# One small job moved from VectorE to ScalarE, the last copies out of PSUM divided between the two, and one last store on GpSimd's queue

## The chip, the cores and the metric

The kernel runs on one core of one Trainium2 chip. The metric is the device time of one execution in microseconds; the time before is the median of three runs, 212.61 us (212.39 to 212.65). Engines are named as in the profile: PE is TensorE, DVE is VectorE, ACT is ScalarE, POOL is GpSimd, SP is SyncE. Each engine works through its own instructions in the order in which the kernel writes them, and waits where an operand isn't ready. A transfer is issued from the queue of SP, ACT or POOL. PSUM is the memory that PE writes its sums to; here it is used as four buffers of two banks each, two with the tag A and two with the tag B.

## The reference

Two independent layers on 2048 positions and 576 channels, their results side by side in the output.

```
# A: 32 heads of 18, each position attends to itself and 7 earlier ones, 2 apart
qkv = x @ wqkv
logits = einsum(q, k[pos - 2*w]) / sqrt(18)      # w = 0..7, masked where pos - 2*w < 0
a = (softmax(logits) weighted sum of v[pos - 2*w]) @ wo

# B: a short shift convolution, a long convolution by FFT, a gate
kv = (sum over t < 4 of k[pos - t] * shift_k[:, t]) * v
y  = irfft(rfft(kv, 4096) * rfft(ssm_k, 4096))[:2048] + kv * ssm_D
b = q * y
out = concat(a, b)
```

## The kernel before

**Layer B.** The 2048 positions are four blocks of 512, and so is the filter ssm_k. For a block i of kv and a block m of the filter the kernel makes a spectrum each (x_spectrum, L776 and L778; filter_spectrum, L627 and L695), as three rows of numbers: two parts and their sum. The output block j is the sum over i of the products of block i with filter block j - i. The products are one DVE multiplication each (L1099). They are summed on PE with identity matrices (sum_of, L1126); the two sums of a block and a third of the channels are copied from PSUM to SBUF by ACT (L1139), and brought back to positions by PE (inverse, L1158 or, for the last third of the last block, last, L1177 and L1185). gate_last multiplies the last block by q on DVE (L1167), in a lower and an upper half of its buffer, and store_b writes each half out as soon as it is made: L1080 the one, L1083 the other in two transfers. The very last of all these sums, for j = 3, t = 2, r = 1, is copied by DVE (L1137) and not by ACT.

**The filter.** Before its spectrum is made each filter block m is folded (fold_filter): two PE groups (L673) into two buffers, two ACT copies of 128x576 (L676) back over the block, and then three accumulating DMAs from POOL's queue (L678, L680, L681). The last of them adds one row of 1x576, the block's row 0 times -0.707, to row 0 of another tile. That signed row is made by negate (L657), for blocks 3 and 2 in the fourth step of the taps' loop, for blocks 1 and 0 between two steps of the attention's logits. Blocks are loaded by transposing DMAs on SP's queue (L227), blocks 3, 2, 1, 0 in this order. L676 overwrites row 0 of blocks 3 and 2, from which their signed rows are made.

**Layer A.** The projections (project, L378, L382, L389, L395; the tail of 64 channels is ct = 4) are copied out of PSUM by ACT (L414). Logits are DVE products (L832) that PE sums (L847); the weighted sum of v is DVE (L956) and PE (L973); the output projection is L1029.

**The order of the work** is written out. PE work that nothing waits for yet stands in a list of units; until() takes as many of them as a table says (PLACES) each time that the kernel waits for a DVE result, need() takes units until a named kind is done. A planner keeps three clocks, D for DVE, P for PE and A for ACT; dve() and pe() advance them. They decide when a gate is due (due) and whether an inverse in the list is ready, and nothing else. The kernel's tile framework adds the waits; it doesn't change the order.

The fourth step of the taps' loop does, in this order: the taps of block 3 on DVE, negate(3, 2), until(), which takes four units, the folds of kv (mirror, L606 on PE into both B buffers and two L609 on ACT), and fold 3, for which need() first takes the units ahead of it.

The store of the last block, by queue: L1080 is issued from SP; of the two L1083 one is issued from ACT and one from SP.

Of the kernel before, what the change touches and what calls it, by code (L numbers as in the profile page):

```python
# [11 lines left out]
ACT = mybir.ActivationFunctionType  # L12
ALU = mybir.AluOpType
# [40 lines left out]
def view(t, offset, dims):  # L54

    return bass.AP(tensor=t.tensor, offset=t.offset + offset, ap=[list(t.ap[0])] + [list(d) for d in dims])
# [3 lines left out]
def kernel(  # L60
# [13 lines left out]
    nc = tc.nc  # L74
    Bsz, S, D = A_x.shape
# [4 lines left out]
    outf = out.flatten_outer_dims()  # L80
# [17 lines left out]
    NBL, BL = 4, 512  # L98
# [20 lines left out]
    def bank2(name, tag):  # L119
        return pp.tile([128, 2, 512], FP32, name=name, tag=tag)  # L120
# [65 lines left out]
    def k_at(m, part):  # L186
        return 3 * HB * (3 - m) + HB * part

    def kTok(m):
        return view(Ks, k_at(m, 2), [[D, 4], [1, D]])  # L190
# [133 lines left out]
    clk = {"D": 0.0, "P": 0.0, "A": 0.0}  # L324
    psum = {"A": deque([0.0, 0.0]), "B": deque([0.0, 0.0])}

    def dve(n, fn, ready=0.0, ns=0.53):

        fn()
        clk["D"] = max(clk["D"], ready) + n * ns / 1000 + 0.125  # L330
        return clk["D"]

    def pe(us, tag, evac, ready=0.0, first=True, last=True):

        clk["P"] = max(clk["P"], ready, psum[tag].popleft() if first else 0.0) + us
        clk["A"] = max(clk["A"], clk["P"] + 0.1) + evac
        if last:
            psum[tag].append(clk["A"])
        return clk["A"]
# [231 lines left out]
    def taps(i):  # L571
        kj, vt = kjs[i], vts[i]
        kv = kv_of(i)
        pair = [view(tB, 4 * D * n, [[D, 4], [1, D]]) for n in range(2)]

        def mult(to, row, n):
            dve(2304 * n, lambda: nc.vector.tensor_tensor(  # L577
                to, view(kj, row * D, [[D, n], [D, 4], [1, D]]), view(skb, row * D, [[D, n], [0, 4], [1, D]]), ALU.mult))

        def add(o):  # L580
            dve(2304, lambda: nc.vector.tensor_tensor(kv, kv if o else pair[0], o or pair[1], ALU.add))

        both = view(tB, 0, [[4 * D, 2], [D, 4], [1, D]])
        if i == 0:
            mult(view(kv, 0, [[4 * D, 1], [D, 4], [1, D]]), 3, 1)
            mult(view(tB, 0, [[4 * D, 1], [D, 4], [1, D]]), 2, 1)
            add(pair[0])
            mult(both, 0, 2)
            add(pair[0])
            add(pair[1])  # L590
        else:
            mult(both, 0, 2)
            add(None)
            mult(both, 2, 2)
            add(pair[0])
            add(pair[1])
        return dve(2304, lambda: nc.vector.tensor_tensor(kv, kv, vt[:], ALU.mult))
# [34 lines left out]
    def row(m, c):  # L632
        return kTok(m)[0:1, c, :]
# [10 lines left out]
    ROOT = 1.4140625  # L644

    def minus_of(m):
        return (view(Ks, k_at(1, 0) + D * (1 + m), [[1, D]]) if m else view(xw, 11 * HB + 2 * D, [[1, D]]))[0:1]

    def spare(m):
        return view(Ks, k_at(1, 0) + D * m, [[1, D]])[0:1]  # L650
# [3 lines left out]
    def negate(*ms):  # L654
        for m in ms:
            signed.add(m)
            dve(288, lambda: nc.vector.tensor_scalar(minus_of(m), spare(m) if m < 2 else row(m, 0), -0.5 * ROOT, None,  # L657
                                                     ALU.mult))

    def fold_filter(m):  # L660
        kt, swapped = kTok(m), m < 2
# [60 lines left out]
    for i in range(NBL):  # L722
        r = taps(i)
        if i == 3:
            negate(3, 2)
# [27 lines left out]
        for n, u in enumerate(mirrors):  # L753
            n = AT[n] if n < 2 else AT[i]
# [153 lines left out]
    logits_run[0] = True  # L908
    sa = softmax(0, view(av, 2048, [[1, 1024]]), view(av, 3072, [[1, 512]]))
    order = [la] * 3 + [partial(negate, 1, 0)] + [la] * 7 + [lb, sa, lb, lb, lb, sa, lb, sa]  # L910
    for n, step in enumerate(order):
        for at in REGROUP:
# [153 lines left out]
    def Y(j, r):  # L1066
        return view(*((av, Y0 + (j % 2) * 8 * D + r * 4 * D) if j else ((av, 0), (xw, 8 * HB))[r]), [[D, 4], [1, D]])
# [4 lines left out]
    def upper(t, j, a, width, c0, n):  # L1072

        return bass.AP(tensor=t.tensor, offset=t.offset + (BL * j + 320 - 64 * a) * width + c0,
                       ap=[[width, 64], [(64, 192)[a] * width, 2], [1, n]])

    def store_b(j, c0, n, src, h):
        other = nc.scalar if j == NBL - 1 else nc.sync
        if h == 0:
            nc.sync.dma_start(outf[BL * j:BL * j + 256, D + c0:D + c0 + n].rearrange("(c p) d -> p c d", c=2), src[:, 0:2])  # L1080
            return
        for a, eng in enumerate((other, nc.sync)):
            eng.dma_start(upper(outf, j, a, 2 * D, D + c0, n), src[64 * a:64 * a + 64, 2:4])  # L1083
# [22 lines left out]
    def sums(j, t, group):  # L1106

        until()
        for i, pr, ready in group:
            out = sum_of(j, t, i, pr, ready)  # L1110
        return out

    def sum_of(j, t, i, pr, ready):

        m = j - i
        for r in range(2):
            sign = ((1, 1), (-1, 1), (-1, -1), (1, -1))[m][r]
            terms = ((2, ident if sign > 0 else identn), (1 - r ^ (m & 1), identn2 if sign > 0 else ident2))
            if i == 0:
                acc[r] = bank2("ps_z", "B")  # L1120
                clk["P"] = max(clk["P"], psum["B"][r])
            for n, (part, w) in enumerate(terms):
                for s in range(2):
                    for h in range(2):
                        o = 64 * ((h + s) % 2)
                        nc.tensor.matmul(view(acc[r], 512 * h, [[192, 2], [96, 2], [1, 96]])[o:o + 64], w[64 * h:64 * h + 64, 64 * h:64 * h + 64],  # L1126
                                         pr[64 * h:64 * h + 64, part, :].rearrange(
                                             "p (a g e) -> p g a e", a=2, g=4)[:, 2 * s:2 * s + 2],
                                         start=(i == 0 and n == 0), stop=(i == j and n == 1),
                                         tile_position=(64 * h, o))  # L1130
            clk["P"] = max(clk["P"], ready) + 0.34
        if i == j:
            for r in range(2):
                y, z = (Y(j, r)[:, :, TH * t:TH * t + TH].rearrange("p (a b) d -> p a b d", a=2),
                        view(acc[r], 0, [[512, 2], [TH, 2], [1, TH]]))
                if (j, t, r) == (NBL - 1, 2, 1):
                    nc.vector.tensor_copy(y, z)  # L1137
                else:
                    nc.scalar.activation(y, z, ACT.Copy)  # L1139
                out = pe(0.0, "B", 0.85)  # L1140
            return out
# [4 lines left out]
    def inverse(j, c0, n, ready):  # L1146
# [17 lines left out]
        def gate_last(lo, hi):  # L1164
            qB = qBs[j][:, :, c0:c0 + n]
            for s, src in enumerate((lo, hi)):
                dve(2 * n, lambda: nc.vector.tensor_tensor(qB[:, 2 * s:2 * s + 2], src, qB[:, 2 * s:2 * s + 2], ALU.mult),  # L1167
                    clk["P"])
                store_b(j, c0, n, qB, s)
# [23 lines left out]
        def back():  # L1193
            ps = bank2("ps_back", "A")
            for src, w in ((A, flip2), (y, flipn)):
                for c in range(2):
                    for h in range(2):
                        o = h ^ (1 - c)
                        nc.tensor.matmul(ps[64 * o:64 * o + 64, 1 - c, 0:n], quarter(w, h, 1),
                                         src[64 * h:64 * h + 64, c], start=(src is A), stop=(src is y),  # L1200
                                         tile_position=(64 * h, 64 * o))
            r = pe(0.0009 * n, "A", ev, box["r"])
            if j == NBL - 1:
                tasks.append((r, partial(gate_last, y[:, 0:2], ps[:, :, 0:n])))
                return
            nc.scalar.activation(y[:, 2:4], ps[:, :, 0:n], ACT.Copy)

            def gate():
                if c0 == 0:
                    return  # L1210
                qB = qBs[j]
                dve(4 * D, lambda: nc.vector.tensor_tensor(qB, yA[:, j % 2, 0:4, :], qB, ALU.mult), r)
                for h in range(2):
                    store_b(j, 0, D, qB, h)
                if j + 2 < NBL:
                    load_q(j + 2)


            (late if j == NBL - 2 else tasks).append((r, gate))
# [126 lines left out]
```

## Time and profile before

| | |
|---|---|
| median of three runs | 212.61 us |
| the profiled execution, whole | 212.5 us |
| its span, first to last instruction | 210.8 us |
| PE, DVE, ACT, POOL busy | 200.1, 193.1, 150.5, 74.0 us |
| granted clock of PE | 0.998 |

The span is shorter than the execution by 1.7 us, which lie around the instructions. A row of the timeline gives the start and the length in us, the engine, the line, the operation, output <- input with its shape, how many were merged into the row, and in brackets how long the engine stood idle before it and whose end ended that. A row of a list of waits gives who waited for whom, us in total, how often, and the longest.

### The profile page before, as it was taken

The page shows a single profiled execution, that of the slowest core. Times are in us where ns is not written, and L with a number is a line of the kernel's source. Part 1 is how long each engine was busy: PE and PEld are TensorE (multiplying, and loading weights), DVE is VectorE, ACT ScalarE, POOL GpSimd, SP SyncE. Part 2 cuts the span into 40 slices and gives each one's busy share as a digit, 9 for nine tenths or more (in the row PEclk, how much of TensorE's full clock was granted, in tenths as well). Part 3 has the DMA queues.
Part 4 walks back from the last instruction along what each step waited for, and adds up shares of the span by engine and source line. Part 5 has one row for each costly group of instructions (what it writes and reads, how often), then busy time and mean ns, then how long its engine had stood idle before and what let it go on. Part 6 is the DMA issues. An engine that isn't in the chain of part 4 may idle for free.

```text
span 210.8 us, 5106 instructions
## 1 busy us (share of the span) xinstructions
PE 200.1 (95%) x2114; PEld 110.7 (53%) x2122; DVE 193.1 (92%) x146; ACT 150.5 (71%) x218; POOL 74.0 (35%) x111
## 2 busy tenths in 40 slices
PE   7999999999999999899999999999989999999891
PEld 2443443344554656564354666656555666666460
DVE  7989999999999999858889999999999849999981
ACT  3799988657684989986369788855666796775540
POOL 8999993001195516320175000002029004033000
PEclk9999999999999999999999999999999999999999
DMA  6999998999639336999999997587559995985133
GB/s 201 303 328 231 266 342 280 170 192 182 151 75 122 48 40 87 180 181 171 235 225 238 194 234 159 105 208 185 153 223 255 239 322 110 214 243 182 28 113 111
DMA packets 35396, 39.66 MB, mean 188 GB/s; under 512 B 17619, under 2 KB 29007, under 8 KB 35374
## 3 DMA queue, kind: packets, MB, share of 16 engines
q1 hardware_dynamic: 26812, 24.88, 47.2%
q0 software_dynamic: 6096, 11.96, 30.4%
q10 hardware_dynamic: 2466, 2.51, 3.5%
q8 instruction: 16, 0.26, 0.5%
q14 instruction: 6, 0.05, 0.1%
HBM read 13.11 MB, written 4.72 MB: 85 GB/s over the span
## 4 chain that ended last, share of the span: by engine, by line
PE 80%; ACT 10%; DVE 5%; issue 2%; DVEq 0%; ACTq 0%
PE ps_proj L378 16%; PE ps_z L1126 9%; PE ps_wo L1029 8%; PE ps_acc L973 7%; PE ps_inv L1158 7%; PE ps_fx L776 6%; PE ps_log L847 4%; PE ps_proj L500 3%; PE ps_fk L627 3%; PE ps_proj L382 3%; PE ps_proj L389 3%; ACT Ks L695 3%; PE ps_rev L673 2%; PE ps_fk L628 1%; ACT qk L977 1%
## 5 line engine op out<-in xcount | busy, mean ns | idle before, releaser
L378 PE MATMUL ps_proj<-xw 128*128 128x512 bf16 x153 | 37.4, 380 | 0.6 <-issue 0.3
L832 DVE TENSOR_TENSOR av<-qk 128x4096 bf16<-128x4096 bf16 (+1 forms) x16 | 31.7, 2013 | 2.8 <-PE ps_log L847 2.8
L378 PEld LDWEIGHTS <-xw 128*128 128x128 bf16 x160 | 14.0, 97 | 20.5 <-issue 6.2
L1099 DVE TENSOR_TENSOR qk<-xw,Ks 128x2304 bf16<-128x2304 bf16 x14 | 18.5, 1355 | 2.5 <-PE ps_inv L1158 2.4
L1139 ACT ACTIVATE av<-ps_z 128x768 bf16<-128x768 f32 x20 | 15.3, 808 | 6.2 <-PE ps_z L1126 6.2
L414 ACT ACTIVATE qk<-ps_proj 128x1024 bf16<-128x1024 f32 x14 | 14.3, 1023 | 7.6 <-PE ps_proj L389 3.3
L695 ACT ACTIVATE Ks<-ps_fk 128x576 bf16<-128x576 f32 x32 | 18.6, 717 | 1.3 <-PE ps_fk L628 1.3
L577 DVE TENSOR_TENSOR tB<-kj,skb 128x4608 bf16<-128x4608 bf16 (+1 forms) x8 | 19.3, 2417 | 0.1
L778 ACT ACTIVATE xw<-ps_fx 128x576 bf16<-128x576 f32 x32 | 18.4, 666 | 0.0
L776 PE MATMUL ps_fx<-xw,TB 128*128 128x288 bf16 x128 | 18.0, 286 | 0.2
L1055 POOL DMA_DIRECT2D Ks<-Ks x3 | 3.7, 1218 | 41.1 <-PE ps_wo L1029 28.7
L1029 PE MATMUL ps_wo<-qk 128*128 128x288 bf16 x128 | 17.8, 287 | 0.0
L627 PE MATMUL ps_fk<-Ks,TB 128*128 128x384 bf16 x62 | 16.9, 326 | 0.8 <-ACT Ks L695 0.7
L414 ACT ACTIVATE v<-ps_proj 128x1024 bf16<-128x1024 f32 x9 | 9.3, 1029 | 9.3 <-PE ps_proj L378 4.3
L973 PE MATMUL ps_acc<-av,ident 64*64 64x512 bf16 x160 | 15.3, 377 | 0.0
L628 PE MATMUL ps_fk<-Ks,TB 128*128 128x192 bf16 x62 | 15.2, 245 | 0.0
L776 PEld LDWEIGHTS <-TB 128*128 128x128 bf16 x128 | 12.0, 97 | 6.0 <-issue 2.9
L1029 PEld LDWEIGHTS <-qk 128*128 128x128 bf16 x128 | 11.6, 98 | 5.6 <-issue 3.0
L1158 PE MATMUL ps_inv<-av,TI 128*128 128x288 bf16 (+1 forms) x96 | 13.6, 293 | 0.6 <-ACT av L1139 0.6
L1161 ACT ACTIVATE v<-ps_inv 128x576 bf16<-128x576 f32 (+1 forms) x14 | 9.5, 677 | 6.3 <-PE ps_inv L1158 6.3
L977 ACT ACTIVATE qk<-ps_acc 128x1024 bf16<-128x1024 f32 x8 | 8.2, 1024 | 8.0 <-PE ps_acc L973 8.0
L956 DVE TENSOR_TENSOR av<-Ks,v 128x4096 bf16<-128x4096 bf16 x6 | 13.6, 2286 | 0.2 <-PE ps_acc L973 0.2
(199 smaller groups left out, 471.3 us busy)
## 6 DMA issues: line engine op xcount, KB each, us to landing
Ks<-Ks POOLq DMA_DIRECT2D x9, 576.0 KB, 7.1
TB<-av SPq DMA_DIRECT2D x12, 256.0 KB, 5.5
kj<-in_B_k_dram SPq DMA_DIRECT2D x6, 504.0 KB, 6.1
vt<-in_B_v_dram SPq DMA_DIRECT2D x8, 288.0 KB, 5.2
Ks<-av SPq DMA_DIRECT2D x8, 256.0 KB, 5.5
Ks<-Ks SPq DMA_DIRECT2D x3, 576.0 KB, 6.1
Ks<-in_A_x_dram SPq DMA_DIRECT2D x2, 576.0 KB, 5.2
xw<-in_A_wqkv_dram SPq DMA_DIRECT2D x2, 576.0 KB, 5.9
```

Of the source, the lines that this page charges most:

```text
L378: nc.tensor.matmul(ps[:, jp, :], wq(kb, comp, 128 * ct, 128), xT(kb, 1024 * jj + 512 * jp, 512), **se)
L414: nc.scalar.activation(view(t, o + pad + 1024 * jj, [[512, 2], [1, 512]]), ps[:], ACT.Copy)
L577: dve(2304 * n, lambda: nc.vector.tensor_tensor(to, view(kj, row * D, [[D, n], [D, 4], [1, D]]), view(skb, row * D, [[D, n], [0, 4], [1, D ...
L627: nc.tensor.matmul(o[:, 0:2], w, rhs[:, 0:2], start=start, stop=stop)
L695: nc.scalar.activation(view(Ks, k_at(m, cs ^ (m & 1)) + 96 * gi, [[768, 3], [384, 2], [1, 96]]), acc3(ps), ACT.Copy, scale=(PSG, MSG)[cs][ ...
L776: nc.tensor.matmul(ps[:, pm, 0:HD], TX[:, 2 * pm + c, 128 * gi:128 * gi + 128], kv[:, 2 * c + pm, HD * h:HD * h + HD], start=(c == 0), sto ...
L832: return P, at, step, dve(1024 * nj, lambda: nc.vector.tensor_tensor(view(P, at, [[step, 4], [256, nj], [1, 256]]), view(t, o + 256 * hh, ...
L973: nc.tensor.matmul(acc[64 * o:64 * o + 64, h, :], ident[64 * h:64 * h + 64, 64 * h:64 * h + 64], view(P, 256 * u, [[2048, 2], [1, 256]])[6 ...
L1029: nc.tensor.matmul(ps[:, r, 0:HD], oT(hh, 2 * c + r, t)[:, o:o + 128], wo[:, t // 2, t % 2, HD * h:HD * h + HD], start=(t == 0 and h == 0) ...
L1099: r = dve(3 * QTR, lambda: nc.vector.tensor_tensor(pr, view(xw, HB * XG[i] + QTR * t, [[HB, 3], [1, QTR]]), view(Ks, k_at(j - i, 0) + QTR ...
L1126: nc.tensor.matmul(view(acc[r], 512 * h, [[192, 2], [96, 2], [1, 96]])[o:o + 64], w[64 * h:64 * h + 64, 64 * h:64 * h + 64], pr[64 * h:64 ...
L1158: nc.tensor.matmul(ps[:, c, 0:n], TI[:, sl, pm, 128 * c:128 * c + 128], Y(j, pm)[:, sl, c0:c0 + n], start=(pm == 0 and sl == 0), stop=(sl ...
```

## The change

Three edits. negate makes its rows with an ACT activation (Copy with a scale) in place of a DVE multiplication, at the same place of the program; the planner's A advances by 0.6 in place of D by 0.28. The two copies of the last sums, for j = 3 and t = 2, are each divided: the first two of the four slices by ACT, the other two by DVE; the two halves lie in different banks of PSUM. And of the last channels of the last block (c0 > 0) the transfer of L1080 is issued from POOL's queue and not from SP's.

```diff
     def negate(*ms):
         for m in ms:
             signed.add(m)
-            dve(288, lambda: nc.vector.tensor_scalar(minus_of(m), spare(m) if m < 2 else row(m, 0), -0.5 * ROOT, None,
-                                                     ALU.mult))
+            nc.scalar.activation(minus_of(m), spare(m) if m < 2 else row(m, 0), ACT.Copy, scale=-0.5 * ROOT)
+            clk["A"] += 0.6
...
     def store_b(j, c0, n, src, h):
-        other = nc.scalar if j == NBL - 1 else nc.sync
+        end = j == NBL - 1
+        other = nc.scalar if end else nc.sync
         if h == 0:
-            nc.sync.dma_start(outf[BL * j:BL * j + 256, D + c0:D + c0 + n].rearrange("(c p) d -> p c d", c=2), src[:, 0:2])
+            (nc.gpsimd if end and c0 > 0 else nc.sync).dma_start(outf[BL * j:BL * j + 256, D + c0:D + c0 + n].rearrange("(c p) d -> p c d", c=2), src[:, 0:2])
             return
...
-                if (j, t, r) == (NBL - 1, 2, 1):
-                    nc.vector.tensor_copy(y, z)
+                if (j, t) == (NBL - 1, 2):
+                    nc.scalar.activation(y[:, 0], z[:, 0], ACT.Copy)
+                    nc.vector.tensor_copy(y[:, 1], z[:, 1])
                 else:
                     nc.scalar.activation(y, z, ACT.Copy)
```

## The prediction

> **What bounds the kernel now.** I read the busy shares of the page first, then who waited for whom on PE and on DVE from 62 us on, then ACT and PE around 46 to 63 us, where the first pair of signed rows is made, and last the timeline from 202 us.
>
> ```profile
> PE 200.1 (95%) x2114; PEld 110.7 (53%) x2122; DVE 193.1 (92%) x146; ACT 150.5 (71%) x218; POOL 74.0 (35%) x111
> ```
>
> All of PE's waits from 62 to 195 us:
>
> ```profile
> PE ps_z L1126 <- ACT qk L977: 0.8, 1, 0.8
> PE ps_fk L627 <- ACT Ks L695: 0.7, 1, 0.7
> PE ps_proj L378 <- issue: 0.3, 2, 0.2
> ```
>
> The longest of DVE's, from 62 to 203 us (in total, times, longest):
>
> ```profile
> DVE av L832 <- PE ps_log L847: 2.8, 3, 1.4
> ```
>
> In 133 us PE waits 1.8 us, and never for DVE; DVE waits for PE. So **PE's order is the bound**: time that PE loses before 62 us is not won back, and time that DVE saves there is worth nothing. Only behind the last product does the end hang on short steps of ACT, DVE and DMA.
>
> **Edit 1: the signed rows on ScalarE.** It removes four L657 instructions from DVE and puts four multiplications of 1x576 into ACT's stream. DVE's rows (ns, first and last start), and ACT's around the first two:
>
> ```profile
> L657 DVE TENSOR_SCALAR Ks<-Ks x3: 290/293/325, 54.6 to 63.3; 1x576 bf16<-1x576 bf16 x3
> ```
>
> ```profile
> L657 DVE TENSOR_SCALAR xw<-Ks x1: 378/378/378, 63.6 to 63.6; 1x576 bf16<-1x576 bf16 x1
> ```
>
> ```profile
> 45.93 1.02 ACT L414 ACTIVATE qk<-ps_proj 128x1024 bf16<-128x1024 f32 x1 [1.03 <-PE ps_proj L389]
> 47.97 1.02 ACT L414 ACTIVATE qk<-ps_proj 128x1024 bf16<-128x1024 f32 x1 [1.02 <-PE ps_proj L378]
> 48.89 1.19 ACT L609 ACTIVATE xw<-ps_fold 128x576 bf16<-128x576 f32 x2
> 50.66 1.02 ACT L414 ACTIVATE qk<-ps_proj 128x1024 bf16<-128x1024 f32 x1 [0.58 <-PE ps_proj L395]
> 51.58 1.19 ACT L609 ACTIVATE xw<-ps_fold 128x576 bf16<-128x576 f32 x2
> 53.45 1.02 ACT L414 ACTIVATE qk<-ps_proj 128x1024 bf16<-128x1024 f32 x1 [0.68 <-PE ps_proj L382]
> 54.97 1.19 ACT L676 ACTIVATE Ks<-ps_rev 128x576 bf16<-128x576 f32 x2 [0.49 <-PE ps_rev L673]
> ```
>
> The trace has no ACT multiplication of one partition; nearest are the copies of 576 elements, two in 1.19, so 0.6 each. DVE saves some 1.3 us (three of 0.3 and 0.38), which is worth nothing by the waits above.
>
> What counts is the **place in ACT's stream**. negate(3, 2) is called after the taps of block 3, ahead of that step's until() and of fold 3. The units popped between it and fold 3's L676 at 54.97 evict, in the kernel's order, as L414, two L609, L414, two L609, L414. Counted back from 54.97, the new instructions stand between the L414 that ends at 46.95 and the one at 47.97. On DVE the same call came behind a long backlog, at 54.6, and nothing was late. On ACT it comes at 46.95, and the row of filter 2 isn't there: its transposing load, the second of L227, is the one issued at 41.3.
>
> ```profile
> L227 SPq DMA_TRANSPOSE Ks<-in_B_ssm_k_dram x1: 3454/3454/3454, 41.3 to 41.3; - x1
> DMA to landing us min/median/max: 9.0/9.0/9.0
> ```
>
> It lands at 50.3. ACT makes row 3 in 0.6 of its 1.02 idle, then **stands from 47.6 to 50.3 before row 2**. Behind that instruction is queued the L414 of 47.97, then the two L609; PE waits for their buffers.
>
> ```profile
> 50.54 0.68 PE L606 MATMUL ps_fold<-xw,fold 128*64 128x288 bf16 x8
> 51.15 0.41 PE L395 MATMUL ps_proj<-xw 64*64 64x512 bf16 x4
> 51.49 1.92 PE L382 MATMUL ps_proj<-xw 128*64 128x512 bf16 x16
> ```
>
> ```profile
> 54.53 0.41 PE L673 MATMUL ps_rev<-Ks,flip 128*128 128x288 bf16 x2 [0.28 <-ACT qk L414]
> ```
>
> ```profile
> 55.67 0.41 PE L673 MATMUL ps_rev<-Ks,flip 128*128 128x288 bf16 x2 [0.25 <-ACT Ks L676]
> ```
>
> ```profile
> 59.73 1.92 PE L382 MATMUL ps_proj<-xw 128*64 128x512 bf16 x16
> ```
>
> Step by step: row 2 runs 50.35 to 50.95; L414 to 51.95; the L609 pair to 53.1. The next folds (L606 of 50.54) use both B buffers that this pair empties, so their second half starts at 53.1 and ends at 53.4. Then the projection unit L395 and L382, which took 51.15 to 53.41, 2.26: to 55.65. Its L414: 55.7 to 56.7. The second L673 group, which needs that buffer and started at 54.53, starts at 56.75: **+2.2**. A hold of 3 us has thus lost what ACT had idle (0.58 and 0.68).
>
> Against it stands a gain. L676 rewrites row 0 of filter 3, which L657 reads, so it waited for DVE: it starts at 54.97, just behind the first L657 (54.6 and 0.29), while L414 had ended at 54.47. PE's 0.25 at 55.67 comes from that. On ACT the order is free, so 0.2 to 0.25 goes: I take -0.2. From there to 59.73 ACT and PE alternate with no slack. Sum on PE at 59.73: 2.2 - 0.2 = **+2.0**, carried to the end. Bounds: the hold can't cost more than its length plus the added work, 3.4 + 0.6 - 1.02 = 3.0; below, it costs nothing if ACT's idle after it takes it up.
>
> ```profile
> 62.17 1.02 ACT L414 ACTIVATE v<-ps_proj 128x1024 bf16<-128x1024 f32 x1 [0.86 <-ACT xw L609]
> 65.27 1.02 ACT L414 ACTIVATE v<-ps_proj 128x1024 bf16<-128x1024 f32 x1 [2.08 <-PE ps_proj L389]
> ```
>
> negate(1, 0) falls between these two in ACT's stream; the second waits 2.08 for PE. Two rows of 0.6 are hidden there, and would cost PE 1.2 without that gap. Their inputs were there for DVE at 63.6, and ACT, 2 us late, comes after that. The planner's clocks change (A +0.6, D less 0.28 a row), but until() pops by count, so I expect PE's and ACT's order unchanged: nothing.
>
> The Trainium skill speaks against the move as such: "ScalarE: Activation LUTs", Rules for kernel authors, says to multiply on VectorE. By its formula (186 ns and 0.833 ns an element) a row would be an estimated 0.67, and the sum 0.07 more. The trace agrees on the sign, 0.6 against 0.25 to 0.38; no row here shows that this, rather than the wait, matters.
>
> **Edit 2: the last copies divided.** The tail on ACT, PE, DVE, PE again and SP:
>
> ```profile
> 202.80 0.81 ACT L1139 ACTIVATE av<-ps_z 128x768 bf16<-128x768 f32 x1 [0.30 <-PE ps_z L1126]
> ```
>
> ```profile
> 205.18 0.49 ACT L1179 ACTIVATE v<-ps_inv 128x384 bf16<-128x384 f32 x1 [0.17 <-PE ps_inv L1177]
> ```
>
> ```profile
> 203.66 1.48 PE L1177 MATMUL ps_inv<-av,TI 128*128 128x192 bf16 x16 [0.26 <-ACT av L1139]
> ```
>
> ```profile
> 203.13 0.96 DVE L1137 CAST av<-ps_z 128x768 bf16<-128x768 f32 x1 [0.91 <-PE ps_z L1126]
> 204.00 0.55 DVE L1167 TENSOR_TENSOR TB<-v,TB 128x768 bf16<-128x768 bf16 x1
> 204.47 0.95 DVE L1167 TENSOR_TENSOR TB<-ps_back,TB 128x768 bf16<-128x768 f32 x1
> 206.19 1.02 DVE L1167 TENSOR_TENSOR TB<-ps_back,TB 128x384 bf16<-128x384 f32 x2 [0.78 <-PE ps_back L1185]
> ```
>
> ```profile
> 205.47 0.70 PE ps_back L1185 x14
> ```
>
> ```profile
> 206.78 0.38 SPq L1080 DMA_DIRECT2D out_dram<-TB  x1
> 207.25 0.59 SPq L1083 DMA_DIRECT2D out_dram<-TB  x1
> ```
>
> Half a copy is 0.49 on ACT (L1179's 128x384) and about 0.5 on DVE (1.02 for two). The first sum, ready at 202.80, is then out at 203.3 on both, not 203.61: the inverse starts at 203.35, -0.3. DVE is through both halves at 203.85, not 204.09, so L1167 at 204.00 and 204.47 moves by -0.25, and with it PE's 205.47, which waits for the buffer that the second of them empties (204.47 + 0.95). ACT's copies move by 0.3, so the gate binds: **-0.25** up to the last L1167. If the two engines hindered each other the bound is 0; L1139 and L1137 overlap by 0.48 now at their full rate.
>
> **Edit 3: the last upper store on GpSimd's queue.** SP is through with L1080 at 207.16, and L1083 waits for the second L1167, whose pair ends at 207.21: SP had no issue time to save. So 0 on the path, and the Trainium skill ("DMA: Bandwidth & Descriptors", Issuing engines are not separate DMA queues) agrees that spreading saves issue time alone. The last two stores (L1083 on SP and on ACT at 207.25) land, in us from issue, least, median and most, so:
>
> ```profile
> DMA to landing us min/median/max: 2.0/2.1/2.3
> ```
>
> That is 209.5 for ACT's, 209.25 shifted. A store from POOL isn't in the trace; its nearest are a 144 KB copy (L736 at 58.0) and the last q load (L1089, issued from 192.4), in this order:
>
> ```profile
> DMA to landing us min/median/max: 2.0/2.0/2.0
> ```
>
> ```profile
> DMA to landing us min/median/max: 3.4/3.4/3.4
> ```
>
> From 206.5 that is 208.5 to 209.9; I take 2.4, near the lone copy, 208.9: hidden. At 3.4 it costs 0.65.
>
> **Sum:** 2.0 - 0.25 + 0 = +1.75 on the profiled execution's 212.5 us (span 210.8): 214.25. The median of the runs is 0.1 above it, so 214.3. Here 0.2% (0.4 us) is about what a measurement tells from no change.
>
> **The rivals.**
>
> *POOL's end is late (chance 0.27).* Behind its last DMA POOL has a drain, and it leads the closing barrier:
>
> ```profile
> L1341 POOLq DRAIN  x1: 5782/5782/5782, 192.7 to 192.7; - x1
> L1341 POOLq EVENT_SEMAPHORE  x4: 17/17/17, 210.1 to 210.7; - x4
> ```
>
> The drain ended at 198.5, 2.1 behind the landing of the last q load (193.0 + 3.4) and 5.5 behind its issue. Now it has 11 us of cover; with a store at 206.5 it has none. By the landing it would end at 211.0, by the issue at 212.0, against 209.8 for the barrier: +1.2 to +2.2 on the forecast, 215.5 to 216.5. Against: the drain may be that long for the three loads or for a cause other than stores.
>
> *The stall is half absorbed (0.12).* If PE or ACT has slack that the rows don't show, behind 60 us, +2.0 becomes 0.5 to 1.3: 212.9 to 213.7. PE's waits speak against it.
>
> *Not slower: no hold (0.10).* By the steps above, each us by which filter 2 lands earlier gives one back; from 48.1 on (50.3 less 2.2) the hold costs nothing, and 0.25 of the removed DVE wait and 0.25 of the tail remain: 212.1. It decides at a landing 2.2 us earlier than the trace's.
>
> *It does nothing that counts (0.03):* hold and gains cancel, 212.6.
>
> Forecast: 0.48. The range 212.8 to 216.3 leaves out the last two and a little of the first. Faster 0.10, same 0.05, slower 0.85.
>
> **What would show it.** Right: ACT idle from about 47.6 to 50.3, its wait put down to the filter load; L414 near 50.9; PE idle between 50.6 and 53.1; L382 of 59.73 near 61.7; L676 no longer behind DVE; the spectral tail the same but 2 us later; L1177 0.3 sooner behind the last sums. Wrong: ACT's new rows standing elsewhere in its stream; PE late at 61.7 but not at 190; a last event on POOL's queue.

## The result, and the profile after

| | before | after |
|---|---|---|
| median | 212.55 us (212.39 to 212.65, 4 runs) | 216.11 us (215.34 to 219.99, 4 runs) |
| profiled execution, and its span | 212.5, 210.8 us | 215.85, 214.2 us |
| busy: PE, DVE, ACT, POOL | 200.1, 193.1, 150.5, 74.0 us | 200.7, 192.5, 152.6, 75.7 us |

The changed kernel is slower: 1.0162 times the time before, 95% interval 1.0137 to 1.0187. The run of 219.99 was disturbed and is left out of that ratio; without it the median after is 215.85. The forecast was 214.3 with a range of 212.8 to 216.3; the case that came is nearest to the rival "POOL's end is late", 215.5 to 216.5. The sum is made on the profiled execution, 215.85 - 212.5 = +3.35 us. In the tail the lines of the changed kernel stand one or two higher: L1080, L1083, L1126, L1158, L1177, L1341 before are L1081, L1084, L1127, L1160, L1179, L1343 after; the divided copies are L1138 on ACT and L1139 on DVE, the gate is L1169.

**The hold.** ACT's timeline of the changed kernel from 46 us on (start, length, instruction; in brackets the idle time before it and what ended it):

```profile
46.84 0.67 ACT L657 ACTIVATE Ks<-Ks 1x576 bf16<-1x576 bf16 x1
49.30 0.68 ACT L657 ACTIVATE Ks<-Ks 1x576 bf16<-1x576 bf16 x1 [1.79 <-DMA Ks<-in_B_ssm_k_dram]
49.89 1.00 ACT L414 ACTIVATE qk<-ps_proj 128x1024 bf16<-128x1024 f32 x1
50.79 1.15 ACT L609 ACTIVATE xw<-ps_fold 128x576 bf16<-128x576 f32 x2
```

The two rows stand where the prediction put them, and ACT waits before the second for filter 2's load. But it waits 1.79 and not 2.7: in this execution the load landed at 49.2, not at 50.3. What PE made of that:

```profile
51.47 0.97 PE L606 MATMUL ps_fold<-xw,fold 128*64 128x288 bf16 x8 [0.86 <-ACT xw L609]
52.37 0.41 PE L395 MATMUL ps_proj<-xw 64*64 64x512 bf16 x4
...
55.74 0.40 PE L673 MATMUL ps_rev<-Ks,flip 128*128 128x288 bf16 x2 [0.28 <-ACT qk L414]
...
56.94 0.41 PE L673 MATMUL ps_rev<-Ks,flip 128*128 128x288 bf16 x2 [0.31 <-ACT Ks L676]
...
61.05 1.92 PE L382 MATMUL ps_proj<-xw 128*64 128x512 bf16 x16
```

Against the rows of before: the second L673 group is +1.21 late (55.74 against 54.53), the one behind L676 +1.27 (56.94 against 55.67), and L382 +1.32 (61.05 against 59.73). PE carries +1.32 from there to 195 us. At 195.9 only 0.91 is left of it, at a place that the prediction's window of waits, 62 to 195 us, had just left out. Before:

```profile
195.28 0.33 PE L1126 MATMUL ps_z<-qk,identn 64*64 64x384 bf16 x4
195.93 0.36 PE L1126 MATMUL ps_z<-qk,ident 64*64 64x384 bf16 x4 [0.32 <-DVE qk L1099]
```

and after, without the wait:

```profile
196.60 0.33 PE L1127 MATMUL ps_z<-qk,identn 64*64 64x384 bf16 x4
196.84 0.36 PE L1127 MATMUL ps_z<-qk,ident 64*64 64x384 bf16 x4
```

196.84 - 195.93 is +0.91. But the missing 0.41 is not won back by the changed kernel; it had been lost in that execution of before. With edit 2 alone (below), whose rows are made on DVE as before, PE keeps to the times of before up to here (195.26 for 195.28) and goes on without the wait:

```profile
195.26 0.33 PE L1126 MATMUL ps_z<-qk,identn 64*64 64x384 bf16 x4
195.51 0.36 PE L1126 MATMUL ps_z<-qk,ident 64*64 64x384 bf16 x4
```

What made DVE late in the execution of before stands earlier in its stream, where the run with edit 2 alone waits 0.22 us:

```profile
170.28 1.36 DVE L1099 TENSOR_TENSOR qk<-xw,Ks 128x2304 bf16<-128x2304 bf16 x1 [2.40 <-PE ps_inv L1158]
```

PE's instructions around it lie within 0.02 us of each other in the two runs, so PE wasn't the cause; what was stays open. The hold thus costs 1.32 against an execution without that loss, and 0.91 against this one.

**The divided copies.** ACT, DVE and PE behind the last sums, after:

```profile
203.71 0.87 ACT L1138 ACTIVATE av<-ps_z 128x384 bf16<-128x384 f32 x2 [0.30 <-PE ps_z L1127]
```

```profile
204.23 1.02 DVE L1139 CAST av<-ps_z 128x384 bf16<-128x384 f32 x2 [1.10 <-ACT av L1138]
205.17 0.55 DVE L1169 TENSOR_TENSOR TB<-v,TB 128x768 bf16<-128x768 bf16 x1
205.64 0.95 DVE L1169 TENSOR_TENSOR TB<-ps_back,TB 128x768 bf16<-128x768 f32 x1
207.38 1.02 DVE L1169 TENSOR_TENSOR TB<-ps_back,TB 128x384 bf16<-128x384 f32 x2 [0.79 <-PE ps_back L1187]
```

```profile
204.85 1.48 PE L1179 MATMUL ps_inv<-av,TI 128*128 128x192 bf16 x16 [0.54 <-DVE av L1139]
```

The halves cost what was expected, two in 0.87 on ACT and in 1.02 on DVE. But they do not stand side by side. DVE has been idle for 1.10 when ACT's first half, 0.49 of the 0.87, ends at 204.20; it starts at 204.23. So the first sum is out at 204.8, 1.1 behind 203.71, where the undivided copy needed 0.81. The inverse starts 1.14 behind the first copy, against 0.86 (202.80 to 203.66) before: +0.28.

**The store and the end.** The last upper store on POOL, with its time to landing:

```profile
208.23 0.73 POOL L1081 DMA_DIRECT2D out_dram<-TB  x1 [13.37 <-DVE TB L1169]
```

```profile
DMA to landing us min/median/max: 2.2/2.2/2.2
```

It lands at 210.4. POOL's and SP's last instructions after, and SP's before (shortest, median and longest in ns, first and last start):

```profile
L1343 POOLq DRAIN  x3: 46/99/5161, 208.2 to 213.9; - x3
L1343 SPq DRAIN  x3: 7/7/13, 211.3 to 213.6; - x3
L1343 POOLq EVENT_SEMAPHORE  x4: 17/17/17, 213.4 to 214.0; - x4
```

```profile
L1341 SPq DRAIN  x3: 7/7/13, 210.0 to 210.3; - x3
```

SP, which waits for all the stores, is at the closing barrier at 211.3 (before: 210.0). POOL comes at 213.4, when a drain of 5161 ns ends that began at 208.2. Before, both came at 210.0 to 210.1. So the drain exposes about 2.05 us.

**The sum:** hold 0.91 (1.32 less the 0.41 that the execution of before had lost itself), divided copies 0.28, last stores 0.16 (SP is 1.35 late, the last gates 207.38 - 206.19 = 1.19), drain 2.0: 3.35.

### The profile page after: what moved, and what is told of

Its sections match the earlier page's. It is cut to its first block, busy times and chain, and to the rows that moved or that the text cites. A ratio compares the mean times of both kernels' runs of the same rounds, so it can differ in the third digit from the quotient of the medians.

```text
span 214.2 us, 5103 instructions
## 1 busy us (share of the span) xinstructions
PE 200.7 (94%) x2114; PEld 111.0 (52%) x2122; DVE 192.5 (90%) x143; ACT 152.6 (71%) x223; POOL 75.7 (35%) x112
## 4 chain that ended last, share of the span: by engine, by line
PE 70%; ACT 9%; issue 9%; DMA 7%; DVE 1%; POOLq 0%; ACTq 0%; DVEq 0%
PE ps_proj L378 13%; PE ps_wo L1029 7%; PE ps_acc L973 7%; PE ps_fx L776 7%; PE ps_z L1127 5%; DMA Ks<-in_B_ssm_k_dram 4%; PE ps_inv L1160 4%; PE ps_fk L627 4%; PE ps_log L847 4%; PE ps_proj L500 3%; ACT Ks L695 2%; DMA out_dram<-TB 2%; PE ps_proj L389 2%; ACT qk L414 2%; PE ps_proj L382 2%
## 5 line engine op out<-in xcount | busy, mean ns | idle before, releaser
L1141 ACT ACTIVATE av<-ps_z 128x768 bf16<-128x768 f32 x19 | 14.5, 808 | 5.5 <-PE ps_z L1127 5.5
L1160 PE MATMUL ps_inv<-av,TI 128*128 128x288 bf16 (+1 forms) x96 | 13.6, 293 | 0.6 <-ACT av L1141 0.6
```

Of the source, the lines that this page charges most:

```text
L1160: nc.tensor.matmul(ps[:, c, 0:n], TI[:, sl, pm, 128 * c:128 * c + 128], Y(j, pm)[:, sl, c0:c0 + n], start=(pm == 0 and sl == 0), stop=(sl ...
```

## The experiments

In all of them the kernel before, run between them on the same chip, stands beside: 212.36, 212.54, 212.24 and 212.25 us in the four series below, in this order: the single edits; the load's place and the early store; the split tiles, the copy on POOL and the early rows; the whole change with the load first. The second and the fourth series ran on chips of their own, the first and the third on the same one.

### Each edit alone

Edit 1 alone: the diff of negate.

> Edit 1 alone: the four signed rows on ScalarE, copies and stores as before. Theory (the wait for filter 2's load holds ACT; the last stage gives part of it back, since DVE's stream sets its pace): PE 1.2 to 1.4 us late at the L382 that follows fold 2, and 0.8 to 1.0 us late at the first of the last sums; time +0.9 us, ratio about 1.004. Rival (PE's delay is carried whole): +1.3 us. Second rival (the rows cost by their work, four of 0.68, wherever they stand): the same time as with the rows placed later.

Edit 2 alone: the diff of the copies.

> Edit 2 alone: the last two copies divided between ACT and DVE, each half in its own bank of one PSUM buffer. Theory (DVE's half waits for ACT's half of the same buffer, so the two don't run side by side): from the first copy to the first inverse 1.14 us in place of 0.86, to the gate 1.46 in place of 1.20; time +0.25 us, ratio about 1.001. Rival (the prediction: halves side by side): -0.25 us.

Edit 3 alone: the diff of store_b.

> Edit 3 alone: the last upper store from POOL's queue. Theory (POOL's drain behind its last DMA ends the kernel): a drain of about 5.1 us from the issue of that store, the closing barrier some 2.0 us later than before although all stores have landed; time +2.0 us, ratio about 1.0095. Rival (the landing of the store): at most +0.1, since the store lands before ACT's and SP's last.

| | median (runs) | ratio to before, 95% |
|---|---|---|
| edit 1 | 215.36 (213.14 to 216.17, 6) | 1.0125, 1.0085 to 1.0165 |
| edit 2 | 212.68 (212.38 to 213.66, 12) | 1.0016, 0.9998 to 1.0033 |
| edit 3 | 214.54 (214.27 to 215.11, 4) | 1.0107, 1.0091 to 1.0123 |

No edit gains. Edit 3 costs 2.2, with the same drain:

```profile
L1341 POOLq DRAIN  x3: 46/99/5160, 207.4 to 213.1; - x3
```

Edit 2's loss is at the edge of what a measurement tells, but the trace has the same wait:

```profile
202.90 1.02 DVE L1138 CAST av<-ps_z 128x384 bf16<-128x384 f32 x2 [1.10 <-ACT av L1137]
```

Edit 1 is the surprise: 0.9 was expected, and it is 3.0 over before by the medians, with a spread of 3 us, while its profiled execution, 213.14, is its fastest. If it is the hold, it must cost far more in other runs than in this trace. (Three of the 23 runs of before lie at 213.15 to 214.59, so single long runs occur without the edit, but not five in six.) The next experiments ask on what it hangs.

### What the hold hangs on

**The same work at another place.** Edit 1, with row 2 made at the head of fold 2's unit and not ahead of fold 3:

```diff
+            if m == 2:
+                negate(2)
...
-            negate(3, 2)
+            negate(3)
```

> Edit 1 with only the place of one row changed: row 3 where edit 1 has it, row 2 made at the head of fold 2's unit, that is between fold 3's two copies and fold 2's on ACT, when filter 2 has long landed. Theory (place, not work): no wait for the load, PE not late at L382 and perhaps 0.25 us early, since fold 3's copies no longer wait for DVE; time within 0.3 us of before, 0 to -0.25. Rival (the rows' work on ACT costs): +0.5 us or more.

Measured: 212.52 (212.49 to 213.04, 11 runs), ratio 1.001, 0.999 to 1.003. Its row 2:

```profile
56.42 0.67 ACT L657 ACTIVATE Ks<-Ks 1x576 bf16<-1x576 bf16 x1
```

Four rows on ACT in 0.67 each, and none of the 3 us, in the same series: the place costs them, not the work. But PE, which was expected on time, is late. ACT's first copy of fold 3 (here L678) starts at 55.34 and not at 54.97, PE waits longer behind it, and L382 comes at 60.15, 0.42 late:

```profile
56.04 0.41 PE L675 MATMUL ps_rev<-Ks,flip 128*128 128x288 bf16 x2 [0.63 <-ACT Ks L678]
```

The medians hardly show it; the fastest runs do, 212.49 here and 212.06 before.

**The same work and place, the load earlier.** Edit 1, and filter 2's load issued ahead of the projection weights:

```diff
-            load_w(nc.sync, 2, raw)
-            for m in range(1, NBL):
+            load_filter(1)
+            load_w(nc.sync, 2, raw)
+            for m in range(2, NBL):
                 load_filter(m)
```

> Edit 1 alone, with filter 2's transposing load issued ahead of the three loads of L154 and L156, so at about 39.4 instead of 41.3. Theory (the hold): what edit 1 costs, and what spreads its runs from 213.1 to 216.2, is ScalarE standing before row 2 until that load lands. With 6.7 to 9.0 us from issue to landing (the four L227 loads before) it lands at 46.1 to 48.4, when ScalarE comes to row 2 (47.5): no wait or one under 0.9, PE within 0.5 of before at L382 (59.73), 212.3 to 212.9 and runs within 1 us of each other. Rival (the rows' work on ScalarE, or another cause of the spread): 214 to 216 and the same spread as with edit 1 alone.

Measured: 212.24 (212.18 to 213.01, 12 runs), ratio 0.9989, 0.9968 to 1.001. Its ACT:

```profile
47.04 1.24 ACT L657 ACTIVATE Ks<-Ks 1x576 bf16<-1x576 bf16 x2
48.18 1.00 ACT L414 ACTIVATE qk<-ps_proj 128x1024 bf16<-128x1024 f32 x1
```

The load landed at 43.4. Both rows run back to back and the wait is gone, and the 12 runs lie within 0.83 us. The 3 us and the spread of edit 1 were seen in the first series, though; in this one edit 1 ran once, at 212.59 (below). That the work on ACT doesn't make them is shown by the late row, in one series with them; that the landing of the load sets the cost is shown by this run and the next, which differ in the order of the loads alone.

**The load later.** Edit 1, and filter 2's load issued behind filter 1's:

```diff
             load_w(nc.sync, 2, raw)
-            for m in range(1, NBL):
-                load_filter(m)
+            load_filter(2)
+            load_filter(1)
+            load_filter(3)
```

> Edit 1 alone, with the second and third of the filter loads behind L154/L156 exchanged: filter 2's load is issued behind filter 1's, at about 44.8 instead of 41.3, and so lands about 3.5 us later, at 51.5 to 54. Theory (the hold): ScalarE stands 4 to 6.5 us before row 2; PE's L382 of 59.73 is 3.5 to 5.5 late, and 217 to 219 comes out, more than 2 above edit 1 alone. Rival (the landing does not set the cost): 215.4 as edit 1 alone, within 0.7. The third filter's accumulating copies come later too, which the theory puts at nothing before 60 us.

Measured: 217.44 (216.82 to 217.44, 4 runs), ratio 1.0224, 1.0179 to 1.0268. ACT, then PE:

```profile
52.12 0.68 ACT L657 ACTIVATE Ks<-Ks 1x576 bf16<-1x576 bf16 x1 [4.54 <-DMA Ks<-in_B_ssm_k_dram]
```

```profile
54.28 1.22 PE L606 MATMUL ps_fold<-xw,fold 128*64 128x288 bf16 x8 [3.60 <-ACT xw L609]
55.43 0.64 PE L395 MATMUL ps_proj<-xw 64*64 64x512 bf16 x4
56.00 2.65 PE L382 MATMUL ps_proj<-xw 128*64 128x512 bf16 x16
```

and by stretches of 2 us (length, PE busy, count, granted clock, DMA share, GB/s):

```profile
52.00:54.00 2.00, 0.00 (x0) 1.00 1.22 261
54.00:56.00 2.00, 1.72 (x12) 0.53 0.46 132
56.00:58.00 2.00, 2.00 (x16) 0.62 0.28 83
58.00:60.00 2.00, 1.72 (x16) 1.00 0.00 0
```

The hold goes as the theory has it, and something comes on top: after 3.60 us without work PE runs at a granted clock of 0.53 and 0.62, L606 takes 1.22 (0.97 in the changed kernel), L395 0.64 (0.41), L382 2.65 (1.92), together 1.21 more.

The Trainium skill ("TensorE: Matmul & The Clock Gate", What's actually happening) says that the array's clock is halved after an idle window of some 3.4 us and let go after a busy one; these rows agree, and in the changed kernel's trace, where PE stood 0.86, the clock stayed at 1.00.

**Edit 1 once more,** the same kernel.

> Edit 1 alone once more, the same kernel: one more pair of a landing of filter 2's load and a time. Theory (the hold): time and landing go together; with a landing at 49.0 the profiled run of edit 1 alone took 213.14, so each us of landing beyond that adds 0.6 to 1 us: 213.8 to 214.2 at 50.0, 215 to 216 at 51.5. Rival: the time is 1 us or more away from this line, and the excess stands in another place of the trace than PE's first wait at 50 to 57 us.

Measured: 212.59, one execution, profiled. Its row 2, and behind it that of the first profile of edit 1:

```profile
48.28 0.68 ACT L657 ACTIVATE Ks<-Ks 1x576 bf16<-1x576 bf16 x1 [0.77 <-DMA Ks<-in_B_ssm_k_dram]
```

```profile
49.06 0.68 ACT L657 ACTIVATE Ks<-Ks 1x576 bf16<-1x576 bf16 x1 [1.55 <-DMA Ks<-in_B_ssm_k_dram]
```

The table adds one more place of PE, the first inverse behind the wait for DVE, in before:

```profile
197.36 1.46 PE L1158 MATMUL ps_inv<-av,TI 128*128 128x384 bf16 x8 [0.58 <-ACT av L1139]
```

| kernel | row 2 starts | PE at L382 | PE at that inverse | profiled execution |
|---|---|---|---|---|
| before | on DVE | 59.73 | 197.36 | 212.5 |
| edit 2 alone | on DVE | 59.72 | 196.94 | 212.38, with edit 2 |
| edit 1, load first | 47.6 | 60.03 | 197.24 | 212.38 |
| edit 1 again | 48.28 | 60.03 | 197.45 | 212.59 |
| edit 1 | 49.06 | 60.81 | 198.02 | 213.14 |
| whole change | 49.30 | 61.05 | 198.27 | 215.85, with edits 2 and 3 |
| edit 1, load late | 52.12 | 65.09 | 202.30 | 217.43 |

From 48.28 on, 0.78 and 0.24 later at row 2 is 0.78 and 0.24 later at L382. The last step is 2.82 at row 2 and 4.04 at L382; the slow clock, 1.21, is the difference. Behind L382 nothing is won or lost: the inverse comes 137.21 or 137.22 later in five of the seven, whether L382 is on time or 5.36 late. The two others are before, with its loss at 195.9, and edit 1 again. And 0.30 stays at L382 with the load first: two rows take 1.24 where ACT had 1.02 idle.

The landing varies: 48.2 and 49.0 in the two profiles of edit 1, 50.3 before, and 48.2 to 51.3 over the eleven profiles of kernels that issue these loads in this order. In the kernel before nothing hangs on it; with edit 1 the time does. The runs of edit 1 at 215 to 216.2 would, at one us for one, need row 2 at 50.9 to 52.1, the last of them later than any of these landings. No profile of such a run was taken: that the landing made them is argued, not shown.

### L676's wait

The kernel before, with the rows left on DVE but row 3 made ahead of the taps of block 3:

```diff
+        if i == 3:
+            negate(3)
         r = taps(i)
...
-            negate(3, 2)
+            negate(2)
```

> The kernel before with the rows left on VectorE, but row 3 made ahead of the taps of block 3 and row 2 behind them. It takes away what L676 at 54.97 waited for (VectorE's L657 of 54.6) without any work on ScalarE. Prediction's step (that wait's end is worth 0.2 to 0.25 to PE, to the end): 212.1 to 212.3. Rival (something else is late there next, as PE's 0.31 before the second L673 with the changed kernel suggests): 212.4 to 212.6, no change.

Measured: 212.35 (212.07 to 214.3, 12 runs), ratio 1.0006, 0.9985 to 1.0028: no change. The profiled execution is the slowest of the twelve; it loses its time behind 62 us, where PE waits 1.6 for DVE. DVE's rows, then PE and ACT:

```profile
L657 DVE TENSOR_SCALAR Ks<-Ks x3: 290/291/431, 44.2 to 63.5; 1x576 bf16<-1x576 bf16 x3
```

```profile
54.56 0.41 PE L673 MATMUL ps_rev<-Ks,flip 128*128 128x288 bf16 x2 [0.28 <-ACT qk L414]
...
55.70 0.40 PE L673 MATMUL ps_rev<-Ks,flip 128*128 128x288 bf16 x2 [0.25 <-ACT Ks L676]
```

```profile
55.00 1.19 ACT L676 ACTIVATE Ks<-ps_rev 128x576 bf16<-128x576 f32 x2 [0.49 <-PE ps_rev L673]
```

The first row is made at 44.2, 11 us ahead of L676, and PE's 0.25 is there as before. L676 starts when the second L673 group's first matmuls are done (54.56 + 0.41 = 54.97), and its row names PE. In the kernel before that was 54.53 + 0.41 = 54.94, DVE's row 54.6 + 0.29 = 54.89: the prediction took the earlier of two ends for the cause. They lie close, and in other executions DVE's comes last: in three of the six profiles with the rows on DVE as before, L676's row names L657, and PE waits 0.33 to 0.43. The longest, with the early store below:

```profile
55.25 1.19 ACT L676 ACTIVATE Ks<-ps_rev 128x576 bf16<-128x576 f32 x2 [0.68 <-DVE Ks L657]
```

### The divided copies without the wait

Edit 2 with the two PSUM tiles of the last sums arranged by halves, so that ACT reads only the one and DVE only the other:

```diff
+                        to, at = (acc[h], 512 * r) if (j, t) == (NBL - 1, 2) else (acc[r], 512 * h)
...
+                    nc.scalar.activation(y[:, 0], view(acc[0], 512 * r, [[TH, 2], [1, TH]]), ACT.Copy)
+                    nc.vector.tensor_copy(y[:, 1], view(acc[1], 512 * r, [[TH, 2], [1, TH]]))
```

> Edit 2 alone, with the last two sums' PSUM tiles arranged by halves instead of by sums: ScalarE reads only the one tile, VectorE only the other. Theory (edit 2 lost 0.27 because VectorE's half waits until ScalarE has read its half of the same tile): the two engines' first copies now start within 0.1 of each other, and VectorE's no longer stands behind ScalarE's; but the first copies wait for the products of both sums, where L1126's second sum came some 0.3 behind the first, so the gate L1167 comes out at -0.1 to +0.1 of before and the whole at 212.3 to 212.6. Rival (the two engines hinder each other in PSUM, or the halves' own fixed cost is what edit 2 lost): copies of 0.6 and more instead of 0.49 and 0.55, the gate late by 0.27 again, 212.6 to 212.9.

Measured: 212.57 (212.44 to 214.11, 12 runs), ratio 1.0016, 0.9998 to 1.0034. ACT, DVE and PE:

```profile
202.77 0.87 ACT L1141 ACTIVATE av<-ps_z 128x384 bf16<-128x384 f32 x2 [0.62 <-PE ps_z L1130]
```

```profile
202.81 1.02 DVE L1142 CAST av<-ps_z 128x384 bf16<-128x384 f32 x2 [0.93 <-PE ps_z L1130]
...
206.23 1.02 DVE L1172 TENSOR_TENSOR TB<-ps_back,TB 128x384 bf16<-128x384 f32 x2 [1.06 <-PE ps_back L1190]
```

```profile
203.69 1.48 PE L1182 MATMUL ps_inv<-av,TI 128*128 128x192 bf16 x16 [0.64 <-ACT av L1141]
```

Now both start together, 0.04 apart, and each keeps its length, 0.87 and 1.02: the engines don't hinder each other, and what held DVE back in edit 2 was the wait that the kernel's framework puts between two engines' reads of one tile. But there is no gain. Each tile now holds a half of both sums, so the first copies wait for the products of both (0.62 idle on ACT, not 0.30), and the last inverse (L1182) comes later: 6.68 behind the inverse of the table above (here at 197.01), where before it was 6.30 and with edit 2 alone 6.57. That is 0.38 lost, as the medians have it (212.57 against 212.24), and not the -0.1 to +0.1 that was expected. The end follows the inverse: the last gates start 2.53 behind it before (203.66 to 206.19), 2.53 after (204.85 to 207.38), and 2.54 here. So the prediction's -0.25 needed the first sum out earlier, and neither arrangement brought that. A tile of its own for each half of each sum might; it wasn't tried, since it needs more PSUM buffers than the two that the sums have.

### POOL's drain

The kernel before, with the first of the last block's two upper stores on POOL instead of the last:

```diff
-            nc.sync.dma_start(
+            (nc.gpsimd if j == NBL - 1 and c0 == 0 else nc.sync).dma_start(
```

> The kernel before, with the first of the last block's two upper stores (issued at about 204.6, columns 0 to 383) on GpSimd's queue instead of the last one. Theory (GpSimd's drain ends about 5 us behind its last DMA's issue, whatever the stores' landing): it ends at 209.7 to 210.3, by the side of SP's 210.0: 212.3 to 212.9, and a drain of 4.5 to 5.5 us in the trace. Rival (a store on that queue costs about 2 us wherever it stands): 214.3 to 214.8, as edit 3 alone (214.54).

Measured: 212.42 (212.14 to 212.99, 10 runs), ratio 0.9997, 0.9976 to 1.0018.

```profile
L1341 POOLq DRAIN  x3: 46/99/5160, 205.2 to 211.0; - x3
L1341 SPq DRAIN  x3: 7/7/13, 210.4 to 210.7; - x3
```

The drain is as long, but it begins at 205.2 and ends at 210.35, when SP arrives at 210.4. The store on that queue is free as long as the last stores cover the drain, here by less than 0.1 us.

The kernel before plus a copy of 16 columns on POOL behind the last lower gate, and no DMA:

```diff
+                if s == 0 and c0 > 0:
+                    nc.gpsimd.tensor_copy(corner[:, 0:16], qB[:, 0, 0:16])
```

> The kernel before plus one small copy on GpSimd (16 columns of VectorE's result) behind the last gate of the lower half, so at about 206.5 to 207.2, and no DMA on its queue (the copy's result is used by nothing). Theory (the drain is long because of a DMA issued on the queue ahead of it): the drain stays short or ends by 210: 212.3 to 212.9. Rival (GpSimd's drain takes some 5 us behind whatever instruction was last): +1.5 to +2.5, 214 to 215, with a drain of about 5 us from 207 on.

Measured: 213.6 (213.55 to 215.13, 4 runs), ratio 1.008, 1.0052 to 1.0107. The theory fell, and the rival is right but for its size:

```profile
206.52 0.20 POOL L1171 COPY corner<-TB 128x16 bf16<-128x16 bf16 x1 [13.49 <-DVE TB L1167]
```

```profile
L1343 POOLq DRAIN  x3: 46/93/4558, 206.5 to 211.6; - x3
```

The drain ends at 211.06, 4.34 behind the copy's end (206.72). In the changed kernel it ends at 213.37, 4.41 behind the end of the DMA's issue (208.96). So it isn't the DMA that makes it long, nor the landing: POOL's last instruction of either kind is followed by some 4.4 us before POOL can close.

### The parts together

The whole change, with filter 2's load first as above.

> The whole change with filter 2's load issued ahead of the loads of L154 and L156, so that ScalarE no longer stands before row 2. Theory (three separate costs): edit 1 without the hold is worth nothing (212.24 against 212.54 with edit 1 alone and this load order), the divided copies 0.27, the store on GpSimd's queue 2.0 to 2.2 by the drain: 214.4 to 215.0, and the runs closer together than the changed kernel's 215.34 to 216.36. Rival (the parts overlap, or part of the drain's cost is owed to the late start of the tail): under 214.0 or over 215.4.

Measured: 214.64 (214.62 to 214.97, 6 runs), ratio 1.0103, 1.0075 to 1.0131. It is in the range that the separate costs give, and the six runs lie within 0.35 us. So of the changed kernel's +3.3 (215.85 against 212.55), 2.4 are what is left with the load first, and the rest, 0.9, is the hold. Alone, the three edits cost 3.0, 0.3 and 2.2 by the medians, which is 5.5 and not 3.3: the long runs of edit 1 alone have no counterpart in the three counted runs of the whole change, and why they were so long is not shown. None of the kernels tried is faster than the one before by more than the measurement tells; the best, edit 1 with the load first, is 212.24 against 212.54, interval 0.9968 to 1.001.

## Why the prediction was right and wrong

- **PE's order is the bound: right.** The delay of 1.32 stood unchanged from 61 to 195 us, and the table shows delays of 0.3 to 5.4 carried whole. But the window of PE's waits ended at 195, and the one wait for DVE, 0.32, ended at 195.93: "never for DVE" was read from a window that stopped too early, and the execution it was read from had lost 0.41 there. The tail of a delay's path has to be read to the end, and the trace of before is one execution too.
- **The place in ACT's stream and the hold: right.** Rows 3 and 2 stand at 46.84 and 49.30, and the order on PE and ACT is unchanged but for them. "Each us by which filter 2 lands earlier gives one back" holds: the load landed 1.05 earlier than the prediction's (row 2 at 49.30 for 50.35), so its 2.2 becomes 1.15, and 1.21 was measured. The failing is that one trace's landing, 50.3, was taken for the kernel's: it varies by 3 us.
- **"-0.2" from L676's wait for DVE: wrong.** PE waited 0.31 there after, 0.25 before, and still 0.25 with the row made at 44.2 on DVE. The row itself named PE. In executions where DVE's row does come last, it is worth up to 0.18 (0.43 against 0.25). Why PE waits 0.31 with the rows on ACT stays open.
- **negate(1, 0) hidden: right.** PE's shift doesn't grow behind 62 us.
- **0.6 a row:** a lone row took 0.67, two in a row 1.24. The estimate by the Trainium skill ("ScalarE: Activation LUTs", What ACT_TABLE_LOAD costs), 0.67, was the better figure for a lone row; the late placement, without the 3 us, shows that this isn't what counted. But the rival "no hold" had the rows' work cost nothing from a landing of 48.1 on, and at 48.2, or with the load first, L382 was still 0.30 late.
- **Edit 2, "-0.25": wrong, +0.28.** The lengths of the halves were right. The step that failed is "the first sum, ready at 202.80, is then out at 203.3 on both": it counted two engines as side by side that read one tile. The stated bound, 0, was no bound either, since a wait of one half for the other wasn't among the costs.
- **Edit 3, the store hidden: right** (landing at 210.4, ahead of the last store).
- **The rival that decided:** POOL's drain ended 5.14 behind the issue of its last DMA, inside the rival's 2.1 (behind the landing) to 5.5 (behind the issue), and close to its upper end. It got 0.27, because the trace of before could not tell which of these it follows. By the runs it follows the end of POOL's last instruction, by 4.3 to 4.4 us behind a single one (4.94 before, behind three loads).

The forecast's middle, +1.75, would have been 2.0 - 0.25; the execution's 3.35 is 0.91 + 0.28 + 0.16 + 2.0. So three terms of the sum were off: the hold too large by a load that landed earlier, the copies of the wrong sign, and the drain put at nothing. The time fell in the range since the rival's price was in it, and it stayed under the upper end because the hold came out small: by the table's one us for one, a landing of 50.3 would have put this execution at 216.9, past the range. That part is luck.

## What to carry to other kernels

Before an instruction is moved to another engine, look up what it waits for and when that is there: in order behind it stands everything else of the engine, and a load that nobody waited for becomes the time and its spread. A copy divided between two engines gains only if the two start together, and no later than the undivided one; look which wait the framework puts between them, and what each tile's readers wait for. Before the last piece of work goes to an engine that had long been done, look at its closing instructions: they start anew behind it.

## What the hardware showed unexpectedly

POOL's closing drain took 4.56 us behind a copy of 0.20 us and 5.16 behind a DMA issue of 0.73, in each case some 4.4 us behind that instruction's end; the ones of SP took 7 to 13 ns. PE's granted clock fell to 0.53 after 3.60 us of idle time in the middle of a kernel, and the three groups of matmuls behind it took 1.21 longer. And the time at which one transposing load landed differed by up to 3.1 us (48.2 to 51.3) between executions with the same loads ahead of it.
